# Loading and turning the first half of an attention stage by head pairs, with its hand-written order rearranged

## The chip, the cores and the metric

One core of one Trainium2 chip runs the whole program. The metric is the device time of one execution in microseconds (us); lower is better. The time before is the median of three runs, 586.37 us (585.89 to 587.06).

## The reference, cut to what is computed

Windowed attention with block summaries (2 batches, 8 heads, 768 positions, 64 numbers per head), then two feed-forward layers (1536 tokens, width 512, inner width 2048), each with its own weights.

```python
k_sum = k.reshape(B, H, 24, 32, 64).max(axis=3)       # one key per 32 positions
v_sum = v.reshape(B, H, 24, 32, 64).mean(axis=3)
scores_l = scale * q @ k.T       # only where |i - j| < 16, else -1e9
scores_s = scale * q @ k_sum.T + log(32)
a = softmax(concat(scores_l, scores_s));  x = a @ concat(v, v_sum)
h = x @ moe_w_in;   x = relu(h)**2 @ moe_w_out
h = x @ moe2_w_in;  x = h * sigmoid(1.702 * h) @ moe2_w_out
```

## The kernel before, in words

**Attention** (lines 377 to 630) works on 12 blocks of 128 query rows, six per batch, and on *units* of two blocks. In the order list each item is one letter and its numbers:

- `k,u,packed` and `q,u,packed` (`load_unit`, 377) load a unit. Packed is one DMA of 512 KB in which a partition holds two neighbouring rows of each head, so that the runs in memory are 512 bytes; unpacked is two DMAs of 256 KB with runs of 256 bytes. `kin` is a ring of three buffers, `q_ring` of two.
- `tk,u` and `tq,u` (`t_k` 489, `t_q` 528, both through `transposed` 462) turn a unit on TensorE with the 128x128 identity, eight products of 128 columns. A packed unit leaves PSUM by four copies of 64 partitions x 512, an unpacked one by two of 128 x 512. `t_k` then takes the maxima of 32 positions (into `ks`) and copies the neighbours' edges; `pk,u` (`put_ks` 519) copies the 24 maxima, once all three units of the batch are there, to both ends of each key window `kw`.
- `sv,b` (`sum_v` 440) loads v of a batch by three packed units into the `kin` ring and sums it by products with the matrix `band`. Four head pairs stand side by side in the array's columns. `ps,b` (`put_vs` 417) copies the sums `vs` into the four buffers of `vw`: two by engine copies, the other two by DMAs that GpSimd issues. `v,i` (`load_vw` 398) loads the value windows of a block, two DMAs of up to 96 partitions with runs of 256 bytes.
- `h,i,e` (`head` 535): with e = 0 the scores of all eight heads of block i (32 records at line 551), the masked minima on VectorE (565) and then the softmax of the even heads; with e = 1 the softmax of the odd heads. The exponentials (574) are on ScalarE, one instruction a head; the sum's reciprocal (588) is on VectorE, and the scaling (581) is on VectorE or GpSimd.
- `t,i` (`tail` 593) turns the probabilities (602), multiplies by the values (614) and splits the result into a rounded part `xh` and a remainder `xl`.

**The first feed-forward layer on the first 512 tokens** (blocks 0 to 3) runs inside the attention stage. `w,f,z` (`prep` 741, `fetch` 683) loads one half of weight block f (z = 0 of `w_in`, z = 1 of `w_out`; 16 blocks, 512 KB a half) and splits it into two parts on ScalarE (699, 730) and VectorE (703, 706, 735). `s,f,half` and `S,f` (`step` 758, `finish` 807) multiply half the tokens or all 512: twelve products at line 768, the activation, and twelve at line 820 into `acc`. The second half of a step is emitted behind the first half of the next one.

**What sets the order.** `ORDER` (27) is read from left to right. Each item adds its operations to `Plan` (113), which places each at the earliest free stretch of its engine (of the DMA queue, for a load) after its inputs, by costs written in the code; `soonest` (194) picks the engine that would end first. All instructions are then emitted by planned start, so that every engine runs its own in that order. An item further left has the first choice of time. `fill` (235) puts products of the identity (`keep_warm`, 1120) into TensorE's planned idle stretches before the first product into `acc3`. Behind the attention stage, `layer`, `pairs` and `late` go through the rest of the two layers.

Of the kernel before, what the change touches and what calls it, by code (L numbers as in the profile page):

```python
# [18 lines left out]
P = 128  # L19
NEG = -8.0e9  # L20

# [6 lines left out]
    m,1 k,2,1 sel w,1,0 m,0 k,1,1 q,1,1 k,0,1 tk,0 tk,1 tk,2 pk,0 q,0,1 sv,0 tq,0 h,1,0 tq,1 m,2 h,1,1 h,0,0  # L28
    w,1,1 pk,1 q,2,0 v,0 h,0,1 ps,0 h,3,0 tq,2 v,1 t,1 h,2,0 v,2 v,3 pk,2 h,2,1 t,0 h,3,1 k,3,0 t,2 s,1,0
    t,3 tk,3 w,2,0 q,3,0 tq,3 k,4,1 tk,4 w,3,0 h,4,0 s,1,1 w,3,1 h,5,0 s,3,0 k,5,0 s,3,1 w,5,0 h,5,1 w,2,1  # L30
    w,0,0 q,4,1 s,2,0 tk,5 w,5,1 S,5 w,9,0 s,2,1 w,6,0 h,4,1 pk,3 w,9,1 v,4 S,9 w,6,1 pk,5 tq,4 w,0,1 t,4
    v,5 h,7,0 w,7,0 s,0,0 t,5 w,7,1 s,0,1 w,4,0 S,7 q,5,1 w,11,0 pk,4 w,4,1 h,6,0 sv,1 S,4 h,7,1 v,6 ps,1
    w,8,0 w,11,1 tq,5 v,7 t,7 S,6 h,6,1 w,10,0 h,8,0 v,8 S,11 h,9,0 h,8,1 t,6 w,8,1 h,9,1 v,9 v,10 w,15,0
    t,8 S,8 w,10,1 S,10 w,12,0 w,12,1 w,15,1 v,11 t,9 h,10,0 w,13,0 S,12 S,15 w,14,0 h,11,0 w,13,1 h,10,1
    S,13 w,14,1 h,11,1 t,10 S,14 t,11
"""
# [219 lines left out]
def kernel(  # L256
# [73 lines left out]
    consts = Buf([], None)  # L330

# [32 lines left out]
    kw_ring = ring(attn, "kw", 4, [P, NPAIR, 2, KW])  # L364
# [12 lines left out]
    def load_unit(dst, src, ring_, u, packed):  # L377
        b, j = divmod(u, NU)
        buf = ring_.take()
        if packed:  # L380
            plan.dma(1.85, lambda: nc.sync.dma_start(
                out=buf.t.rearrange("p (h r d) -> p h r d", h=H, r=2),
                in_=src[b, :, j * UNIT:(j + 1) * UNIT, :].rearrange("h (p r) d -> p h r d", r=2)), writes=[(buf, 0)])
# [8 lines left out]
    def load_k(u, packed=False):  # L392
        load_unit(kin, k, kin_ring, u, packed)

    def load_q(u, packed=False):
        load_unit(qin, q, q_ring, u, packed)

# [63 lines left out]

    def transposed(src, dst):


        buf, packed = src
        w, at = dst
        for n in range(2):
            ps = banks.take()

            def go(n=n, ps=ps):  # L470
                for a in range(4):
                    c0 = (2 * a + n) * P if packed else (a % 2) * H * D + (2 * n + a // 2) * P
                    nc.tensor.transpose(ps.t[:, a * P:(a + 1) * P], buf.t[:, c0:c0 + P], ident)

            op("PE", 0.46, go, reads=[(buf, 0), (consts, "ident")] + ([] if packed else [(buf, 1)]), writes=[(ps, 0)])
            if not packed:
                copy(lambda n=n: at(slice(0, P), slice(2 * n, 2 * n + 2)),
                     lambda ps=ps: ps.t.rearrange("p (a i t) -> p a i t", a=2, i=2), ps, [(w, ("own", 2 * n))])
                w.writer["own", 2 * n + 1] = plan.ops[-1]
                continue  # L480
            for i in range(2):
                copy(lambda n=n, i=i: at(slice(n * D, n * D + D), slice(0, NPAIR)).rearrange(
                    "p a z (t i) -> p a z t i", i=2)[:, :, :, :, i],
                     lambda ps=ps, i=i: ps.t[i * D:i * D + D, :].rearrange("p (a z t) -> p a z t", a=4, z=2),
                     ps, [(w, ("own", 2 * n + i))], cost=0.59)

    OWNS = [("own", x) for x in range(4)]

    def t_k(u):
# [5 lines left out]
        zero = [(0, NSUM)] if j == 0 else [(1, OWN + P)] if j == NU - 1 else []  # L495
        for i, c0 in zero:
            op("POOL", 0.2, lambda i=i, c0=c0: nc.gpsimd.memset(w.t[:, :, i, c0:c0 + EDGE], 0.0),
               writes=[(w, (i, "l" if c0 == NSUM else "r"))])
        transposed(kin[u], (w, lambda rows, ps: w.t[rows, ps, :, OWN:OWN + P]))
        for z in range(2):  # L500
# [4 lines left out]
               reads=[(w, x) for x in (OWNS if kin[u][1] else OWNS[2 * z:2 * z + 2])], writes=[(ks[b], (j, z))])  # L505
# [651 lines left out]
```

## Time and profile before

| | |
|---|---|
| median of three runs | 586.37 us (585.89 to 587.06) |
| span of the profiled execution, first to last instruction | 584.6 us |
| the profiled execution's own time | no figure beside the span is given; the span is 1.8 us under the median |
| TensorE busy | 571.6 us (98%) |
| VectorE busy | 480.4 us (82%) |
| ScalarE busy | 441.8 us (76%) |
| GpSimd busy | 65.8 us (11%) |
| granted TensorE clock | 1.00 throughout (the 2.4 GHz level) |
| chain that ended last | 86% TensorE, 5% ScalarE, 4% VectorE, 3% DMA |
| moved by DMA | 95.79 MB, 164 GB/s over the span |

A busy share is an average over stages with different limits, and TensorE's includes the products of the identity. Matmul ends are modelled, so neighbouring records overlap; the distance from one start to the next tells more than a record's length. In the rows, L is a line of the kernel, `x` the number of instructions, and "idle before, releaser" what an engine waited for.

### The profile page before, as it was taken

The numbers are of one execution on the slowest core, as the hardware profiler recorded it, in microseconds if no ns is written. First come the engines' busy times: TensorE is split into PE (matmuls) and PEld (weight loads), VectorE is DVE, ScalarE is ACT, GpSimd is POOL, SyncE is SP. The second block draws the span as 40 slices with busy tenths as digits, with TensorE's granted clock in tenths as the row PEclk, the third lists the DMA queues.
The fourth block names the chain that finished last, engine by engine and source line by source line (L and its number), as shares of the span: only waits on it lengthen the run. The fifth ranks groups of instructions, "written<-read, shape, count | busy, mean of one in ns | idle before, by whom it ended". The sixth has DMA issues, their size and how long they took to land.

```text
span 584.6 us, 9824 instructions
## 1 busy us (share of the span) xinstructions
PE 571.6 (98%) x3440; PEld 474.3 (81%) x3440; DVE 480.4 (82%) x1040; ACT 441.8 (76%) x909; POOL 65.8 (11%) x125
## 2 busy tenths in 40 slices
PE   7899999999999999999999999999999999999997
PEld 6789888788878888888888888888878888888885
DVE  4899998799889998878888899899998898877421
ACT  5899889999888658888888867676587777778322
POOL 5323113112100000100000000000100002000000
PEclk9999999999999999999999999999999999999999
DMA  9999889555446624444444546633465455545001
GB/s 251 238 237 239 243 260 255 148 172 180 148 148 191 201 71 143 143 145 145 145 145 143 180 145 211 186 112 104 148 181 177 152 178 174 178 163 200 0 1 72
DMA packets 87505, 95.79 MB, mean 164 GB/s; under 512 B 29504, under 2 KB 74560, under 8 KB 87456
## 3 DMA queue, kind: packets, MB, share of 16 engines
q1 hardware_dynamic: 87264, 94.78, 54.1%
q0 software_dynamic: 192, 0.39, 0.4%
q8 instruction: 27, 0.44, 0.3%
q14 instruction: 22, 0.18, 0.1%
HBM read 91.62 MB, written 3.15 MB: 162 GB/s over the span
## 4 chain that ended last, share of the span: by engine, by line
PE 86%; ACT 5%; DVE 4%; DMA 3%; SPq 1%; issue 1%; POOL 0%; DVEq 0%; ACTq 0%
PE acc L996 13%; PE acc L820 13%; PE acc L822 11%; PE m L996 10%; PE m L822 9%; PE h L768 6%; PE m L820 6%; PE h L996 3%; PE acc L768 3%; PE m L768 3%; PE h L822 3%; PE h L820 2%; ACT sm L574 2%; PE m L614 2%; DMA kin<-in_k_dram 1%; DMA kin<-in_v_dram 1%
## 5 line engine op out<-in xcount | busy, mean ns | idle before, releaser
L730 ACT CAST w<-xw 128x512 fp32r<-128x512 f32 (+1 forms) x167 | 97.9, 602 | 20.1 <-DVE xw L706 12.8
L735 DVE TENSOR_TENSOR w<-xw,w 128x512 fp32r<-128x512 f32 (+1 forms) x163 | 107.5, 672 | 5.9 <-ACT w L730 4.0
L706 DVE SCALAR_TENSOR_TENSOR xw<-raw,xw 128x512 uint32<-128x512 uint32 x148 | 101.5, 695 | 5.6 <-ACT raw L699 1.8
L699 ACT ACTIVATE raw<-raw 128x512 f32<-128x512 f32 x148 | 96.1, 675 | 10.9 <-DMA raw<-in_moe_w_out_dram 6.3
L820 PE MATMUL acc<-gh,w 128*128 128x512 f32 (+1 forms) x288 | 82.3, 369 | 0.4 <-DVE w L735 0.2
L703 DVE TENSOR_SCALAR xw<-raw 128x512 uint32<-128x512 uint32 x148 | 65.8, 449 | 6.2 <-DMA raw<-in_moe_w_out_dram 5.8
L820 PEld LDWEIGHTS acc<-gh,w 128*128 128x128 f32 x288 | 51.7, 188 | 9.9 <-DVE w L735 0.5
L822 PE MATMUL acc<-w,gh 128*128 128x512 f32 x192 | 59.1, 389 | 0.0
L768 PE MATMUL h<-xh,w 128*128 128x512 f32 (+1 forms) x184 | 55.6, 363 | 0.6 <-DVE st L588 0.6
L820 PE MATMUL acc<-gl,w 128*128 128x512 f32 (+1 forms) x144 | 52.7, 366 | 0.0
L996 PE MATMUL acc<-top,w 128*128 128x512 f32 x192 | 48.3, 391 | 0.0
L822 PE MATMUL m<-w,gh 128*128 128x512 f32 x148 | 45.7, 390 | 0.0
L735 DVE TENSOR_TENSOR gl<-gs,gh 128x512 fp32r<-128x512 f32 x32 | 22.1, 691 | 28.5 <-ACT gh L730 27.8
L730 ACT CAST gh<-gs 128x512 fp32r<-128x512 f32 x32 | 19.9, 622 | 33.5 <-PE acc L822 25.4
L735 POOL TENSOR_TENSOR w<-xw,w 128x512 fp32r<-128x512 f32 x17 | 22.9, 1344 | 195.9 <-ACT w L730 170.2
L996 PEld LDWEIGHTS acc<-top,w 128*128 128x128 f32 x192 | 35.8, 188 | 8.5 <-ACT r L309 1.2
L822 PEld LDWEIGHTS acc<-w,gh 128*128 128x128 f32 x192 | 36.0, 188 | 7.5
L768 PEld LDWEIGHTS h<-xh,w 128*128 128x128 f32 x184 | 33.3, 189 | 6.3 <-ACT sm L574 0.8
L822 PE MATMUL acc<-w,gl 128*128 128x512 f32 x96 | 37.4, 389 | 0.0
L574 ACT ACTIVATE sm<-sm,st 128x120 f32<-128x120 f32 x96 | 36.6, 383 | 0.0
L996 PE MATMUL m<-top,w 128*128 128x512 f32 x138 | 35.0, 391 | 0.0
L996 PE MATMUL acc<-xh,w 128*128 128x512 f32 x100 | 34.0, 389 | 0.0
(188 smaller groups left out, 1201.8 us busy)
## 6 DMA issues: line engine op xcount, KB each, us to landing
raw<-in_moe_w_out_dram SPq DMA_DIRECT2D x88, 512.0 KB, 3.8
raw<-in_moe_w_in_dram SPq DMA_DIRECT2D x60, 512.0 KB, 3.9
vw<-in_v_dram SPq DMA_DIRECT2D x20, 192.0 KB, 5.8
kin<-in_v_dram SPq DMA_DIRECT2D x6, 512.0 KB, 7.0
out_dram<-r SPq DMA_DIRECT2D x12, 256.0 KB, 2.1
kin<-in_k_dram SPq DMA_DIRECT2D x4, 512.0 KB, 6.0
qin<-in_q_dram SPq DMA_DIRECT2D x4, 512.0 KB, 7.1
qin<-in_q_dram SPq DMA_DIRECT2D x4, 256.0 KB, 6.8
```

Of the source, the lines that this page charges most:

```text
L574: nc.scalar.activation(out=s.t[:, h, :], in_=s.t[:, h, :], func=AF.Exp, bias=st.t[:, 0, h:h + 1], scale=-1.0, accum_out=st.t[:, 1, h:h + 1])
L614: nc.tensor.matmul(ps.t[e * D:(e + 1) * D, p * P + c * HALF:p * P + (c + 1) * HALF], lhsT=vw[i].t[:, c, h * D:(h + 1) * D], rhs=t.t[:, h, ...
L699: nc.scalar.activation(out=top, in_=top, func=AF.Prelu, scale=-(2.0 ** -80), alpha=-(2.0 ** -32))
L703: op("DVE", 0.36, lambda: nc.vector.tensor_scalar(out=x.t, in0=raw.t[:, :, 0], scalar1=29, scalar2=None, op0=ALU.logical_shift_right), rea ...
L706: op("DVE", 0.64, lambda: nc.vector.scalar_tensor_tensor(out=x.t, in0=raw.t[:, :, 1], scalar=3, in1=x.t, op0=ALU.logical_shift_left, op1=A ...
L730: plan.soonest([("ACT", 0.09 + 0.44 * fr, False, lambda: nc.scalar.copy(out=hi.t[:, hc], in_=src())), ("DVE", 0.05 + 0.4 * fr, True, lambd ...
L735: eng.tensor_tensor(out=lo.t[:, lc], in0=src(), in1=hi.t[:, hc].bitcast(F32), op=ALU.subtract)
L768: nc.tensor.matmul(hp.t[:, cols], lhsT=w.t[:, kc * P:(kc + 1) * P], rhs=x.t[:, kc, cols], start=(kc == 0 and n == 0), stop=(kc == KC - 1 a ...
L820: nc.tensor.matmul(a.t[:, cols], lhsT=w.t[:, j * P:(j + 1) * P], rhs=g.t[:, cols], **st)
L822: nc.tensor.matmul(a.t, lhsT=g.t[:, j * P:(j + 1) * P], rhs=w.t, **st)
L996: nc.tensor.matmul(bank.t, lhsT=a, rhs=rhs(b, kh), start=(begin and k == 0 and n == 0), stop=(k == 1 and n == 2), skip_group_check=True)
```

## The change

- k of batch 0 comes as four head pairs (`K,p`, `load_kp`) in place of three units: one DMA of 393 KB, 96 partitions, each with eight neighbouring rows of two heads in runs of 2 KB. `T,p` (`t_kp`) turns a pair by two groups of eight products of 64 columns (96 moving), takes each group out by one copy of 128 x 384, forms the maxima in one reduction and writes edges and maxima for all six blocks at once. The four `kw` buffers become one tile.
- v of batch 0 for the sums comes the same way (`V,p`, `sum_vp`): four loads in the `kin` ring, each summed by eight products that follow each other in the same 24 columns, and one copy of 24 x 128. Batch 1 keeps `sv,1`.
- A new mode packed = 2 (used by `q,0,2`): two loads of four heads, turned by products of 64 columns, out by copies of 128 x 256.
- The softmax goes by two head pairs (heads 0 to 3, 4 to 7) in place of even and odd heads. `g,i,g` (`head_half`) computes the scores of two pairs alone; blocks 0 and 1 use it, the rest `h`. Buffers are tracked per pair.
- `ORDER` is another list. In it q,4 and q,5 are unpacked, k,3 and k,5 packed. The items `W`, `L` and `F` are defined and not used; with `BACK` = 6 and no `L` the later layers' order is the same as before.

```diff
 ORDER = """
+    sel selw K,3 w,3,0 m,0 m,1 m,2 K,0 K,1 q,1,1 q,0,2 T,0 w,1,0 T,3 T,1 K,2 tq,0 T,2 w,2,0 tq,1 g,0,0 g,1,0
+    V,0 g,0,1 v,0 g,1,1 h,2,0 V,1 V,2 v,1 v,2 V,3 k,3,1 ps,0 t,0 k,5,1 h,3,0 q,2,0 h,3,1 w,3,1 t,1 s,3,0
+    h,2,1 tk,3 w,1,1 v,3 t,2 t,3 w,0,0 k,4,1 w,0,1 tq,2 q,3,0 s,1,0 s,1,1 s,0,1 s,3,1 v,4 h,4,0 w,5,0 w,2,1
...
+    def load_pair(src, p):
+        buf = kin_ring.take()
+        plan.dma(1.2, lambda: nc.sync.dma_start(
+            out=buf.t[0:ROWS].rearrange("p (h x) -> p h x", h=2),
+            in_=src[0, 2 * p:2 * p + 2].rearrange("h (p r) d -> p h (r d)", r=RUN)), writes=[(buf, 0)])
...
+    def sum_vp(p):
+        buf = load_pair(v, p)
+        ps = banks.take()
+
+        def go():
+            x = buf.t[0:ROWS].rearrange("p (h r d) -> p h r d", h=2, r=RUN)
+            for r in range(RUN):
+                nc.tensor.matmul(ps.t[0:NSUM, 0:P], lhsT=band_w, rhs=x[:, :, r, :], start=(r == 0), stop=(r == RUN - 1))
...
+    def t_kp(p):
...
+        buf = kpair[p]
...
+        for g in range(2):
+            ps = banks.take()
+
+            def go(g=g, ps=ps):
+                for r in range(4):
+                    for x in range(2):
+                        c0 = (x * RUN + 4 * g + r) * D
+                        nc.tensor.matmul(ps.t[x * D:(x + 1) * D, r * ROWS:(r + 1) * ROWS], lhsT=buf.t[0:ROWS, c0:c0 + D],
+                                         rhs=ident[0:ROWS, 0:ROWS], start=True, stop=True)
...
-    def head(i, e):
+    def scores(i, gs):
...
-            for h in range(e, H, 2):
+            for h in range(4 * g, 4 * g + 4):
```

## Rows read from the trace of the kernel before

**Rows 1.** Busy time by stretch: length, then PE, PEld, DVE, ACT, POOL, clock, DMA, GB/s
```profile
0.00:13.00 13.00, 9.32 (x63) 8.65 (x64) 5.46 (x9) 6.64 (x10) 7.83 (x43) 1.00 0.95 246
13.00:20.00 7.00, 5.91 (x113) 4.54 (x116) 5.52 (x19) 5.44 (x10) 0.59 (x3) 1.00 1.19 308
20.00:36.20 16.20, 13.10 (x225) 11.61 (x217) 14.56 (x78) 15.33 (x65) 5.75 (x12) 1.00 1.10 202
36.20:45.00 8.80, 8.72 (x132) 7.87 (x136) 7.58 (x15) 8.70 (x27) 3.35 (x8) 1.00 0.95 266
45.00:84.00 39.00, 38.12 (x356) 34.14 (x345) 36.06 (x110) 35.73 (x96) 9.41 (x19) 1.00 0.87 240
84.00:165.00 81.00, 80.81 (x757) 66.16 (x756) 70.22 (x198) 71.42 (x187) 16.14 (x24) 1.00 0.64 184
```

**Rows 2.** The products of the identity, line 1123: duration, first and last start
```profile
L1123 PE MATMUL warm<-ident x80: 275/275/579, 1.4 to 35.3; 128*128 128x128 f32 x80
```

**Rows 3.** Timeline of TensorE: the first product of the feed-forward layer
```profile
36.18 0.35 PE L768 MATMUL h<-xh,w 128*128 128x256 f32 x1 [0.62 <-DVE st L588]
```

**Rows 4.** The chain that ended last, up to the first feed-forward step: start, length, what
```profile
4.03 7.92 DMA kin<-in_k_dram
...
13.11 6.01 DMA kin<-in_v_dram
...
21.01 4.54 ACT sm L574 x24
...
32.27 1.10 PE m L614 x32
...
35.34 0.69 DVE xl L627
```

**Rows 5.** The same chain further on: what one piece of TensorE's work takes
```profile
92.14 1.44 PE m L452 x48
...
111.72 2.72 PE acc L820 x12
...
145.49 0.98 PE m L551 x32
...
152.18 0.87 PE m L602 x8
...
164.88 2.72 PE h L768 x12
```

**Rows 6.** Busy time by stretch, columns as in rows 1: three stretches with few kinds of load
```profile
9.00:12.00 3.00, 1.82 (x18) 1.63 (x16) 2.74 (x5) 2.03 (x4) 0.85 (x5) 1.00 1.22 290
24.50:29.00 4.50, 4.25 (x37) 4.05 (x37) 3.64 (x9) 4.33 (x17) 1.72 (x4) 1.00 1.23 199
41.90:44.90 3.00, 3.00 (x62) 2.60 (x63) 2.43 (x5) 2.99 (x7) 1.25 (x2) 1.00 1.12 352
```

**Rows 7.** Groups by line and form, ScalarE and VectorE: busy us, mean ns, idle before
```profile
L309 ACT COPY kw<-acc 64x512 f32<-64x512 f32 x5 | 3.1, 621 | 1.5 <-PE acc L473 1.4
L309 ACT COPY qT<-acc 128x512 f32<-128x512 f32 x1 | 0.6, 585 | 0.0
L782 ACT ACTIVATE r<-h 128x256 f32<-128x256 f32 x2 | 0.8, 380 | 0.2 <-PE h L768 0.2
L502 DVE TENSOR_REDUCE ks<-kw 128x16 f32<-128x512 f32 x6 | 3.8, 681 | 0.8 <-ACT kw L309 0.7
L309 ACT COPY vs<-m 24x128 f32<-24x128 f32 x3 | 0.8, 257 | 1.8 <-PE m L452 1.4 <-DVE vs L310 0.4
L424 ACT COPY vw<-vs 24x512 f32<-24x512 f32 x1 | 0.6, 617 | 0.0
```

**Rows 8.** The page's groups by line: two of the five instructions that split a weight half
```profile
L699 ACT ACTIVATE raw<-raw 128x512 f32<-128x512 f32 x148 | 96.1, 675 | 10.9 <-DMA raw<-in_moe_w_out_dram 6.3
...
L703 DVE TENSOR_SCALAR xw<-raw 128x512 uint32<-128x512 uint32 x148 | 65.8, 449 | 6.2 <-DMA raw<-in_moe_w_out_dram 5.8
```

**Rows 9.** The page's DMA issues: KB each, median us from issue to landing
```profile
vw<-vs POOLq DMA_DIRECT2D x4, 96.0 KB, 5.5
```

More of the change, by code (lines that the diff above doesn't have):

```diff
@@ L481, in transposed @@
[L481 to L487, printed above, removed]
+                    if packed < 2:
+                        c0 = (2 * a + n) * P if packed else (a % 2) * H * D + (2 * n + a // 2) * P
+                        nc.tensor.transpose(ps.t[:, a * P:(a + 1) * P], buf.t[:, c0:c0 + P], ident)
+                        continue
@@ L574, in ex, with softmax @@
+    def softmax(i, g):
+        s, st = sms[i]
+        hs = slice(4 * g, 4 * g + 4)
+        mine = [(s, (x, g)) for x in range(2)]
+        def ex():
+            for h in range(4 * g, 4 * g + 4):
                 nc.scalar.activation(out=s.t[:, h, :], in_=s.t[:, h, :], func=AF.Exp, bias=st.t[:, 0, h:h + 1],
@@ L676, in layer @@
                 prep(m, f)
-            step(m, t, f, 0, TT, [n == 0] * 2, [n == len(order) - 1] * 2)
+            step(m, t, f, 0, TT, [fresh and n == 0] * 2, [n == len(order) - 1] * 2)
             if n >= 2:
@@ L1074, in part, with more, drain @@
         steps[:] = count
+    mores = []
+    def more(f):
+        step(1, 0, f, 0, TT, [not mores] * 2, [False] * 2)
+        mores.append(f)
+    def drain():
+        while pending:
+            finish()
     todo = dict(
-        k=load_k, q=load_q, v=load_vw, tk=t_k, tq=t_q,
+        K=load_kp, T=t_kp, V=sum_vp, g=head_half, q=load_q, k=load_k, v=load_vw, tk=t_k, tq=t_q,
         h=head, t=tail, ps=put_vs, pk=put_ks, sv=sum_v, w=lambda f, z: prep(0, f, f % RING, (z,)),
@@ L1088 @@
     used = [int(item.split(",")[1]) for item in ORDER.split() if item[:2] in ("s,", "S,")]
-    keep_w.update((0, f) for f in sorted(blocks.values(), key=lambda f: used[::-1].index(f))[:2])
+    if not any(item[:2] == "L," for item in ORDER.split()):
+        keep_w.update((0, f) for f in sorted(blocks.values(), key=lambda f: used[::-1].index(f))[:2])
     attn_ops = []
@@ L1100 @@
     end_attention()
+    if not mores:
+        drain()
+    early.clear()
     plan.lean = 1.5, 0.25
     banks.release(banks.last["h0"])
-    while pending:
-        finish()
     parted.add((0, 0))
@@ L1108 @@
     two = list(range(NF))
-    layer(1, 0, two[:1:-1][:10], operands_first(0, 1, 2, *one[:2]))
+    rest = [f for f in two[:1:-1] + two[1::-1] if f not in mores]
+    layer(1, 0, rest[:-BACK], operands_first(0, 1, 2, *one[:2]), not mores)
     pairs(0, 1, 2, one)
```

219 lines of the change are left out of this document (149 added, 70 removed).

## The prediction

> **What bounds the kernel now.** I read the busy time by stretch first. From 36.2 us on TensorE idles for almost nothing: 8.72 of 8.80 us, 38.12 of 39, 80.81 of 81 [rows 1]. Part of what stands before that is no work: the products of the identity run from 1.4 to 35.3 us [rows 2]. The first product of the feed-forward layer starts at 36.18 us [rows 3]. So the total is roughly that moment, plus the useful TensorE work still open at it, plus the holes in what follows.
>
> The holes I get from the prices of single pieces, since records overlap. Tile 0 of the first layer is 16 steps of 2 x 2.72 us [rows 5], 87.0 us. After 36.2 there remain eight of twelve blocks' scores at 0.98 (7.8), 20 of 24 groups of turned probabilities at 0.87/2 (8.7), ten products with the values at 1.10 [rows 4] (11.0), six units of k and q (48 products of 128 columns, which I price as those of the probabilities, 0.109 each: 5.2) and batch 1's sums, 1.44 [rows 5]. That is 121.1 us. The next layer's first product starts at 164.88 [rows 5], 128.7 us after 36.18, so some 7.6 us are holes or overhead. Half steps and switches of array shape explain part, so I count at most 5 us as recoverable.
>
> VectorE and ScalarE are nearly full as well: 14.56 and 15.33 of 16.2 us between 20.0 and 36.2, still about nine tenths later [rows 1]. In the first 20 us they stand: ScalarE works 12.1 us of them, VectorE 11.0 [rows 1]. There the chain waits for loads: the third k unit lands at 11.95 us and the third v unit at 19.12, and the exponentials run from 21.01 [rows 4]. The queue is the reason: in 9 to 12 us, packed loads alone, it moves 290 GB/s, and the stretch of 256-byte runs 199 [rows 6].
>
> **The change, part by part.** *Loads.* A unit of 524 kB takes 524/290 = 1.81 us, a weight half at the rate of the weights' stretch (352 GB/s) 1.49 us, the value windows of an inner block, 393 kB in two loads, at 199 GB/s 1.98 us [rows 6]. A 2 KB run is in no load of before. Its bounds: the packed rate would give 393/290 = 1.36 us for a pair, the weights' 1.12, and the only loads with 96 partitions, those of 256-byte runs, 1.98 [rows 6]. I take 1.12, because the weights' runs (1 and 4 KB) enclose 2 KB. Eight pairs then cost 9.0 us where six units cost 10.9.
>
> *When the last v pair lands.* Before, four units and one weight half (8.7 us of moving) end at 11.95 [rows 4], so the queue starts 3.2 us late. In the new list V3 comes behind seven pairs, three weight halves, q1 and q0, and the windows of blocks 0 to 2 (three times 1.98, less 0.2 for the cut edge of the first: 5.8). With V3 this is 9.0 + 4.5 + 3.6 + 5.8 = 22.9, and V3 lands at 26.1 us, seven later than v before. K2 and the v pairs wait on SyncE for slots of the ring of three, and the loads listed behind them wait too. K2's slot is free once K3 is turned, V0's and V1's once K0 and K1 are, several loads before their turn, so I cost this at nothing; a queue that ran dry would show the 3.2 us of its start again. SyncE issues three loads more in all (two k and v pairs, a half of q0; the four units that change form cancel), beside transfers that last longer.
>
> *From V3 to the first step.* Eight products that no longer stand side by side are 16 records of 0.109 (1.7 us), the copy 0.26, two rounds of copies into `vw` at 0.6 [rows 7] (GpSimd, VectorE and ScalarE share them): 29.3 us. From the first product with the values to the first step it was 36.18 - 32.27 = 3.9 us [rows 3, 4]. So the first step starts at 33.2 us by this chain. If the engines rather than V3 set it, later: I take 33.6, a gain of 2.6 us.
>
> *Copies.* Twelve copies of 64 x 512 at 0.62 (7.4 us) become eight of 128 x 384, between 0.38 and 0.585 [rows 7], say 0.49: 3.9. For q0 four at 0.62 become four at 0.38: 1.0 saved. The reductions move the same elements (six of 0.68 against four, which I put at 1.0), and eight small copies of maxima replace six: nothing. Some 4.5 us of two full engines are saved. GpSimd, 7.83 of the first 13 us busy [rows 1], gets three instructions for `band_w` and copies edges eight times instead of ten; the first edges are wanted near 12 us, so this costs nothing either. Softmax by pairs keeps every instruction and its shape; the packed and unpacked units change places and cancel. Products of 64 columns cost TensorE two records where a turned block had one, at most 16 x 0.109 = 1.7 us a group of a pair; these lie where the identity products lie now [rows 2] and cost nothing, while one of them late on K1 would delay the first scores by about 1 us.
>
> *Scores earlier.* The first scores need K0, K1 and half of q0, the sixth load: 3.2 + 3 x 1.12 + 1.49 + 1.81 + 0.91 = 10.8 us, against 13.8 for all of k, q1 and q0 before. With turning and maxima, exponentials can start near 14.5 instead of 21.01. This fills the empty first 20 us of ScalarE, and it is why I think that V3 and not the softmax comes last before the first tail.
>
> *What is given back.* q2 is turned before 36.2 now, and after the first step in the new list: 8 x 0.109 = 0.9 us of TensorE work, as said. With the load order it is also later. Blocks 2 and 3 use the sums that GpSimd's DMAs bring 5.5 us after their issue [rows 9]: from about 28.1, so near 34; that half of the tokens can be ready near 39, and is not what holds the steps.
>
> *Holes.* With 4.5 us less on two full engines and a queue that moves k and v of batch 0 in 1.9 us less, I take back 1.0 of the 5 us.
>
> *Sum.* -2.6 + 0.9 - 1.0 = -2.7 us on a span of 584.6: 581.9. The median of the runs stands 1.8 us above that span, and I put the difference on it: 586.4 - 2.7 = **583.7 us**. Both ends: a first step at 33.2 with all holes gone gives -3.0 + 0.9 - 5.0 = -7.1; the load at 1.98 us makes V3 6.9 us later, and -2.6 + 0.9 + 6.9 = +5.2.
>
> **The rivals.** *Slower: the pair loads leave part of the queue's engines without work.* A pair fills 96 of 128 partitions. If the moving went by partitions, it would run at three quarters of the rate: 1.12/0.75 = 1.49 us a pair, 8 x 0.37 = 3.0 us later for V3, and -2.6 + 0.9 + 3.0 = +1.3 without the gain in holes: 587.7 us. It decides from 1.33 us a pair on, where 8 x 0.21 eats the 1.7. For it: the loads of 96 partitions were in the slowest stretch, 199 GB/s. Against it: these have 256-byte runs, which explains the rate, and the queue's busy share there is no lower (1.23) than for packed loads (1.22) [rows 6]. The Trainium skill, page "DMA: Bandwidth & Descriptors", section "Rules for kernel authors", asks for 128 partitions and at least 1 MiB in a DMA for full bandwidth, which speaks against loads of 96 partitions and 393 kB. The same page, on why a DMA increments its semaphore by 16, lets a tile of 96 partitions use all 16 engines, and by that part the pair costs 1.12; the equal busy shares fit it.
>
> *The same: weights are late.* At the first step only first halves (w3, w1, w2) are there. The second half of block 3 comes behind V3, k3, k5, q2 (2.6 us at 199 GB/s) and itself: 26.1 + 1.8 + 1.8 + 2.6 + 1.5 = 33.8 us, and its split is five instructions of 0.45 to 0.7 [rows 8], so 37 us on full engines. Between 33.6 and 37 TensorE then has twelve half products of two steps, q2, k3 and the tails. If these are not ready either, 2 to 3 us of new holes take the gain: 586.2 us. For it: the engines are full at that time; against it: five pieces of other work stand in the list there.
>
> *Much faster: the holes go.* If ScalarE and VectorE are what makes the holes, starting their work six us earlier closes them: the -7.1 above, 579.3 us, and up to 581.9. Against it: the splits and exponentials left are the same, and after 84 us both engines have slack [rows 1] and TensorE has not.
>
> **How the numbers follow.** The forecast, a gain of 1.3 to 4.5 us, 0.44; much faster 0.17; the same 0.21; slower 0.18. A difference of 0.2% (1.2 us) is about what a measurement can tell. So faster 0.61, same 0.21, slower 0.18. The range leaves out a tenth at each end: 580.0 to 588.3, which takes in the pair load at 1.5 us and most of the closed holes; 1.98 us a pair lies outside.
>
> **What would show it.** Right: V3's eight products start near 26 us, the first product of the feed-forward layer (line 768 now) starts at 33 to 34.5 us, and TensorE idles no more after it than now; the stretch of k pairs shows well over 290 GB/s. Exponentials begin near 14.5 us. Wrong: V3 after 28 us; a first step after 35 us; or identity products gone earlier but holes of over 2 us between 34 and 45 us, with splits of weights as releasers. If the first step comes before 32 us and the total does not follow, supply and not the start was the bound.

## The result, and the profile after

The changed kernel takes **590.59 us** (median of four runs, 589.69 to 591.61), against 586.42 of the kernel before in the same session: the ratio is 1.0065 with a 95% interval of [1.0047, 1.0083]. The profiled execution took 590.84 us, its span is 588.9 us. Slower by 4.2 us where 2.7 us of gain were forecast, and outside the range.

The busy time by stretch, columns as in [rows 1]:

```profile
0.00:13.00 13.00, 11.03 (x104) 10.29 (x106) 3.88 (x7) 4.86 (x8) 8.50 (x43) 1.00 0.93 240
13.00:20.00 7.00, 6.83 (x117) 5.76 (x114) 4.61 (x22) 5.59 (x12) 0.44 (x2) 1.00 1.15 243
20.00:36.20 16.20, 13.03 (x175) 10.75 (x174) 12.37 (x69) 12.48 (x57) 2.92 (x10) 0.94 1.19 216
36.20:45.00 8.80, 8.05 (x109) 7.53 (x109) 6.41 (x14) 8.13 (x26) 3.90 (x9) 0.92 1.10 237
```

VectorE and ScalarE work *less* up to 36.2 us than before (20.9 and 22.9 us against 25.5 and 27.4 of [rows 1]). The 4.5 us of copies that the prediction saves are about half of this; for the rest, they have not got what they should work on. While K0 and K1 land, the queue moves 258 GB/s, where well over 290 was the sign that the prediction is right:

```profile
8.30:9.90 1.60, 1.60 (x21) 1.52 (x22) 1.11 (x2) 0.24 (x1) 1.18 (x5) 1.00 1.16 258
```

The chain that ended last, from the first v pair on (start, length, what; a DMA's length is from issue to landing, and the loads queued ahead of it land within it):

```profile
11.25 10.09 DMA kin<-in_v_dram
...
26.14 7.08 DMA kin<-in_v_dram
...
33.27 2.82 PE acc L496 x16
```

In [rows 4] the third v unit had landed at 19.12 us. Here the fourth v pair is issued at 26.14 and its products (line 496) start at 33.27. TensorE's timeline shows what this makes of the two moments on which the sum was built, the first product of the feed-forward layer (line 884 now; [rows 3]) and the next layer's first:

```profile
4.47 1.55 PE L562 MATMUL acc<-ident,kin 96*64 96x96 f32 x16 [0.54 <-DMA kin<-in_k_dram]
8.38 2.83 PE L562 MATMUL acc<-ident,kin 96*64 96x96 f32 x32
18.19 0.88 PE L562 MATMUL h<-ident,kin 96*64 96x96 f32 x16
18.90 0.83 PE L562 MATMUL acc<-ident,kin 96*64 96x96 f32 x16
33.27 2.82 PE L496 MATMUL acc<-kin,band_w 96*24 96x128 f32 x16 [2.06 <-DMA kin<-in_v_dram]
43.88 0.39 PE L884 MATMUL h<-xh,w 128*128 128x256 f32 x1
...
169.41 0.39 PE L884 MATMUL h<-xh,w 128*128 128x512 f32 x1
```

The next layer's first product in the kernel before:

```profile
164.72 0.39 PE L768 MATMUL h<-xh,w 128*128 128x512 f32 x1
```

The first product comes at 43.88 instead of 36.18 (+7.7), the next layer at 169.41 instead of 164.72 (+4.7; the chain's piece of it, 164.88 in [rows 5], starts 0.2 later than the first record). Between the two moments lie 125.5 us now, 128.5 before: three of the 7.7 us come back. Twelve more products that turn probabilities are done by then (64 left of 96 where 76 were left; 12 x 0.109 = 1.3 us), and the rest is fewer holes. From the next layer's first product to the end it is 419.5 us, before 419.9. So in this execution the whole loss arises ahead of the first feed-forward product. The longest waits there of ScalarE, VectorE and TensorE all go back to the last v pair (waits from 20 to 45 us: engine, line, what for; total, times, longest):

```profile
ACT vs L310 <- PE acc L496: 3.0, 1, 3.0
DVE vw L451 <- ACT vs L310: 3.0, 1, 3.0
PE acc L496 <- DMA kin<-in_v_dram: 2.1, 1, 2.1
```

Two theories stood against each other. **Loads:** a load on 96 partitions takes longer than one on 128 whatever its runs, and eight of them put the last v pair off. **Clock:** there are 24 products of the identity left where 80 stood [rows 2]; 32 records of line 562 take 2.83 us at 8.38 us, at the lower level (1.2 GHz), and 1.5 us at 18.19 at the upper (2.4 GHz); and the windows show 0.94 and 0.92 from 20 to 45 us, where the engine had just idled 2.06 us for the last v pair. (The windows print 1.00 from 0 to 13 us all the same, and so does the table of the kernel before; the lengths of the records tell otherwise. An identity product takes 421 ns or more up to 8.03 us here, and mostly 275 from 19.9 on. In the kernel before, 14 of them stand without a gap up to 4.36 us, 421 ns or more each, and from 6.07 on they take 275.) Two more were tried: that an earlier start is lost to late weights anyway (**supply**), and that the **list** does not fit.

### The profile page after: what moved, and what is told of

Read it like the earlier page. It is cut to its first block, busy times and chain, and to the rows that moved or that the text cites. A ratio compares the mean times of both kernels' runs of the same rounds, so it can differ in the third digit from the quotient of the medians.

```text
span 588.9 us, 9991 instructions
## 1 busy us (share of the span) xinstructions
PE 578.0 (98%) x3528; PEld 481.1 (82%) x3528; DVE 480.5 (82%) x1043; ACT 439.1 (75%) x906; POOL 61.7 (10%) x122
## 4 chain that ended last, share of the span: by engine, by line
PE 91%; DMA 5%; ACT 1%; DVE 1%; issue 0%; POOL 0%; POOLq 0%; DVEq 0%
PE acc L936 13%; PE acc L1112 13%; PE acc L938 11%; PE m L1112 10%; PE m L938 9%; PE h L884 8%; PE m L936 6%; PE h L1112 4%; PE acc L884 3%; DMA kin<-in_v_dram 3%; PE m L884 3%; PE h L938 3%; DMA raw<-in_moe_w_in_dram 2%; PE h L936 2%; PE m L729 2%; PE m L717 1%
## 5 line engine op out<-in xcount | busy, mean ns | idle before, releaser
L850 DVE TENSOR_TENSOR w<-xw,w 128x512 fp32r<-128x512 f32 (+1 forms) x171 | 115.3, 683 | 6.7 <-ACT w L845 3.5
L821 DVE SCALAR_TENSOR_TENSOR xw<-raw,xw 128x512 uint32<-128x512 uint32 x148 | 102.7, 699 | 7.6 <-ACT raw L814 3.5
L818 DVE TENSOR_SCALAR xw<-raw 128x512 uint32<-128x512 uint32 x148 | 63.6, 435 | 12.9 <-DMA raw<-in_moe_w_in_dram 10.2
L1112 PE MATMUL acc<-top,w 128*128 128x512 f32 x186 | 47.1, 391 | 0.0
L845 ACT CAST gh<-gs 128x512 fp32r<-128x512 f32 x32 | 19.9, 623 | 35.0 <-PE h L938 25.4
L938 PE MATMUL acc<-w,gl 128*128 128x512 f32 x96 | 37.4, 389 | 0.0
L884 PE MATMUL h<-xl,w 128*128 128x512 f32 (+1 forms) x92 | 32.5, 353 | 0.0
```

Source lines behind the costliest of these rows:

```text
L818: op("DVE", 0.36, lambda: nc.vector.tensor_scalar(out=x.t, in0=raw.t[:, :, 0], scalar1=29, scalar2=None, op0=ALU.logical_shift_right), rea ...
L821: op("DVE", 0.64, lambda: nc.vector.scalar_tensor_tensor(out=x.t, in0=raw.t[:, :, 1], scalar=3, in1=x.t, op0=ALU.logical_shift_left, op1=A ...
L845: plan.soonest([("ACT", 0.09 + 0.44 * fr, False, lambda: nc.scalar.copy(out=hi.t[:, hc], in_=src())), ("DVE", 0.05 + 0.4 * fr, True, lambd ...
L850: eng.tensor_tensor(out=lo.t[:, lc], in0=src(), in1=hi.t[:, hc].bitcast(F32), op=ALU.subtract)
L884: nc.tensor.matmul(hp.t[:, cols], lhsT=w.t[:, kc * P:(kc + 1) * P], rhs=x.t[:, kc, cols], start=(kc == 0 and n == 0), stop=(kc == KC - 1 a ...
L938: nc.tensor.matmul(a.t, lhsT=g.t[:, j * P:(j + 1) * P], rhs=w.t, **st)
```

## The experiments

All medians against the kernel before on the same chip; since that one takes 586.4 to 587.5 us there, the ratios compare better than the medians. "V" is where the last v sum's products start, "first" the first feed-forward product, "next" the next layer's first, each in us of the profiled execution. That execution lies within 1.6 us of its median, except in v6_same, where it is 2.7 us above it.

| run | what differs from the changed kernel | median | ratio, 95% interval | V | first | next |
|---|---|---|---|---|---|---|
| (changed) | | 590.59 | 1.0065 [1.0047, 1.0083] | 33.3 | 43.9 | 169.4 |
| v_first | v pairs listed ahead of the windows | 591.92 | 1.0090 [1.0059, 1.0122] | 26.7 | 38.9 | 170.0 |
| v_units | v of batch 0 in three units | 590.25 | 1.0055 [1.0038, 1.0072] | 25.7 | 36.7 | 168.8 |
| v_units_w31 | the same, one weight half earlier | 591.26 | 1.0074 [1.0050, 1.0098] | 25.9 | 36.7 | 168.6 |
| old_list | the order of before, so no pair load at all | 589.37 | 1.0035 [1.0019, 1.0050] | 20.3 | 40.7 | 168.4 |
| dense | denser products of the identity | 590.35 | 1.0059 [1.0036, 1.0082] | 33.9 | 43.1 | 168.0 |
| k_units | k of batch 0 in three units | 591.75 | 1.0065 [1.0042, 1.0088] | 31.0 | 42.8 | 169.3 |
| price | pair load planned at 1.6 us | 592.65 | 1.0095 [1.0071, 1.0120] | 34.0 | 41.7 | 170.8 |
| refit_pairs | pair load planned at 1.7 us, list rearranged | 593.63 | 1.0121 [1.0088, 1.0155] | 31.1 | 40.9 | 172.2 |
| refit_units | no pair load, list rearranged | 588.87 | 1.0028 [1.0013, 1.0043] | 29.3 | 42.1 | 167.2 |
| v6 | v pairs on 128 partitions | 587.12 | 1.0011 [0.9990, 1.0031] | 30.5 | 39.3 | 165.6 |
| v6_same | the same, and the plan of the changed kernel | 585.38 | 0.9976 [0.9965, 0.9987] | 32.8 | 41.6 | 166.7 |
| v6_dense | v6_same with denser products of the identity | 585.46 | 0.9973 [0.9961, 0.9985] | 29.5 | 38.2 | 162.6 |
| refit_v6 | v pairs on 128 partitions, list rearranged | 584.97 | 0.9967 [0.9953, 0.9981] | 27.9 | 36.6 | 163.4 |
| refit_v6_dense | the same with denser products | 584.82 | 0.9972 [0.9961, 0.9983] | 28.8 | 37.4 | 163.0 |

**Loads alone.** Two kernels of nothing but loads, twelve of a form in a row.

```diff
+FORMS = [(8, 128, 128, "r512p128"), (8, 96, 128, "r512p96"), (2, 128, 512, "r2kp128"), (2, 96, 512, "r2kp96"),
+         (1, 128, 1024, "r4kp128"), (1, 96, 1024, "r4kp96"), (16, 128, 64, "r256p128"), (16, 96, 64, "r256p96")]
...
+            nc.sync.dma_start(out=t[0:p].rearrange("p (x r) -> p x r", x=x),
+                              in_=flat[o0:o0 + x * p * r].rearrange("(x p r) -> p x r", x=x, p=p))
```

> Only loads: twelve each of eight forms, runs of 512 B, 2 KB, 4 KB and 256 B, each on 128 partitions (512 KB) and on 96 (384 KB); the attention and both layers are left out and the output is zeros. Partition theory (96 of 128 partitions leave part of the queue idle): every form takes the same time on 96 as on 128 partitions, so the pair form (2 KB, 96) takes what 2 KB on 128 takes, about 1.4 us. Run theory (the runs alone set the rate): the 96 form takes 0.75 of the 128 form, the pair form about 1.1 us. Contention theory (the pair load is slow only beside other loads): the pair form alone takes 1.1 us as well, and the 1.4 to 2.0 us between landings in the changed kernel come from its neighbours.

Busy time by stretch, each stretch inside one form, in the order of the list (length, VectorE, GpSimd, clock, DMA share, GB/s):

```profile
7.00:20.00 13.00, 1.23 (x8) 0.00 (x0) 1.00 1.15 346
23.00:36.00 13.00, 1.47 (x10) 0.00 (x0) 1.00 1.24 279
41.00:54.00 13.00, 1.54 (x10) 0.00 (x0) 1.00 1.05 404
57.00:70.00 13.00, 1.36 (x10) 0.00 (x0) 1.00 1.06 278
74.00:86.00 12.00, 1.39 (x9) 0.00 (x0) 1.00 1.03 416
90.00:102.00 12.00, 1.35 (x9) 0.00 (x0) 1.00 1.02 281
108.00:124.00 16.00, 1.23 (x8) 0.00 (x0) 1.00 1.20 272
130.00:140.00 10.00, 0.93 (x7) 0.00 (x0) 1.00 1.17 256
```

On 128 partitions (every other row) the rate follows the run: 272 GB/s with 256 bytes, 346 with 512, 404 with 2 KB, 416 with 4 KB. On 96 it stays near 280 from 512 bytes on: the 2 KB runs buy nothing. And the DMA share is the same for both, 1.05 at 404 GB/s and 1.06 at 278. The pair form takes 393/278 = 1.41 us with nothing beside it, so the run theory and the contention theory, which expected 1.1, fail. What was expected of the partitions, the same time on 96 as on 128, holds at 2 KB roughly (1.41 us against 524/404 = 1.30), and not with 256 bytes (393/256 = 1.54 against 524/272 = 1.93). Each load kernel ran once. Later the second kernel, with the pair as it is, the same 393 kB on 128 partitions, the packed unit and half a block's windows:

```diff
-FORMS = [(8, 128, 128, "r512p128"), (8, 96, 128, "r512p96"), (2, 128, 512, "r2kp128"), (2, 96, 512, "r2kp96"),
-         (1, 128, 1024, "r4kp128"), (1, 96, 1024, "r4kp96"), (16, 128, 64, "r256p128"), (16, 96, 64, "r256p96")]
+FORMS = [(2, 96, 512, "pair96"), (2, 128, 384, "pair128"), (8, 128, 128, "unit"), (8, 96, 64, "window")]
```

> Loads alone, twelve in a row of each form, everything else left out (the output is zeros): a pair on 96 partitions with runs of 2 KB, the same 393 kB on 128 partitions with runs of 1.5 KB, a packed unit of 524 kB, and value windows (96 partitions, 256-byte runs, 196 kB). Load theory: 1.4 us a load for the first, 0.95 to 1.05 for the second (390 to 410 GB/s), 1.5 for the unit, and under 0.85 for the windows. Rival, the bytes set the time: the first two agree within 5%.

VectorE's timeline, a copy behind each load, two neighbours of each form (the difference of their starts is one load):

```profile
9.40 0.15 DVE L31 COPY acc<-pair 96x1 f32<-96x1 f32 x1 [1.47 <-DMA pair<-in_k_dram]
11.06 0.15 DVE L31 COPY acc<-pair 96x1 f32<-96x1 f32 x1 [1.51 <-DMA pair<-in_k_dram]
...
26.45 0.15 DVE L31 COPY acc<-pair 128x1 f32<-128x1 f32 x1 [0.90 <-DMA pair<-in_k_dram]
27.49 0.15 DVE L31 COPY acc<-pair 128x1 f32<-128x1 f32 x1 [0.89 <-DMA pair<-in_k_dram]
...
40.33 0.15 DVE L31 COPY acc<-unit 128x1 f32<-128x1 f32 x1 [1.65 <-DMA unit<-in_k_dram]
42.14 0.15 DVE L31 COPY acc<-unit 128x1 f32<-128x1 f32 x1 [1.65 <-DMA unit<-in_k_dram]
...
61.97 0.15 DVE L31 COPY acc<-window 96x1 f32<-96x1 f32 x1 [0.88 <-DMA window<-in_k_dram]
63.00 0.15 DVE L31 COPY acc<-window 96x1 f32<-96x1 f32 x1 [0.88 <-DMA window<-in_k_dram]
```

Over the twelve it is mostly 1.64 us for the pair, 1.05 for the same bytes on 128 partitions, 1.81 for the unit (which is what it took in the kernel before, [rows 6]), 1.03 for half a block's windows. Pair and unit are 16 and 20% slower than in the first load kernel, which ran on another chip (393/278 = 1.41 and 524/346 = 1.51), so only ratios within one run count: four pairs cost 6.6 us where three units cost 5.4.

**The order of the v loads.** First the v pairs before the value windows, then v in units.

```diff
-    V,0 g,0,1 v,0 g,1,1 h,2,0 V,1 V,2 v,1 v,2 V,3 k,3,1 ...
+    V,0 V,1 V,2 V,3 g,0,1 v,0 g,1,1 h,2,0 v,1 v,2 k,3,1 ...
```

> The changed kernel with its four v pairs listed together ahead of the value windows. Order theory (V3 is late because the windows of blocks 0 to 2 and the slots stand before it): V3 lands 4 to 5 us sooner than 33.2, the first feed-forward product starts near 40 instead of 43.9, total 587 us. Load theory (the pair loads themselves are slow): V3 lands sooner too, but by less than 3 us since V1 to V3 still wait for slots, and the windows land later; total 588.5 to 590.5.

```diff
-    V,0 g,0,1 v,0 g,1,1 h,2,0 V,1 V,2 v,1 v,2 V,3 k,3,1 ...
+    sv,0 g,0,1 v,0 g,1,1 h,2,0 v,1 v,2 k,3,1 ...
```

> The changed kernel with v of batch 0 by the three packed units and the band sums of before, at the place of the first v pair. Load theory: three units at 1.81 replace four pairs at 1.5 to 1.7, the last lands near 26 us, its sum takes 0.64 instead of 2.8, the first feed-forward product starts by 38, total 585 to 587 us. Order theory: as v_first within 1 us, since both have v ahead of the windows.

Both bring the first product forward, by 5.0 and 7.2 us, and both give it back: the next layer comes 131.1 and 132.2 us after it. Neither total was expected by any theory: v in units, its last sum at 25.7 us, is as slow as the changed kernel. The waits of TensorE in v_units, from 36 to 48 us, are on the value windows and on copies of k:

```profile
PE m L729 <- DMA vw<-in_v_dram: 1.2, 2, 0.6
...
PE acc L515 <- DVE kw L311: 0.8, 1, 0.8
```

So an early start alone is worth nothing here. Whether one weight half is the cause was tried next.

```diff
-    ... tq,0 T,2 w,2,0 tq,1 ... h,3,1 w,3,1 t,1
+    ... tq,0 T,2 w,3,1 tq,1 ... h,3,1 w,2,0 t,1
```

> The kernel with v of batch 0 in packed units (it reached the first feed-forward product at 36.7 us and gave all of it back in holes), now with the second half of weight block 3 listed where the first half of block 2 stood, and the other way round. Supply theory (the holes after an early first step are products that wait for second halves): the second product group of block 3 starts before 41 us instead of 47, the next layer begins at 166 to 167 us instead of 168.84, the median is 587.5 to 588.5. Rival, the list as a whole (every engine's order is placed for other costs, no single load is the cause): the next layer stays at 168.5 or later and the median at 590 or above.

Next layer 168.6 and a median of 591.26, as the rival said: this load is not the cause of the holes. Other single loads were not tried, and what would close them stays open.

**The order of before.**

```diff
-    sel selw K,3 w,3,0 m,0 m,1 m,2 K,0 K,1 q,1,1 q,0,2 T,0 w,1,0 T,3 T,1 K,2 tq,0 T,2 w,2,0 tq,1 g,0,0 g,1,0
+    m,1 k,2,1 sel w,1,0 m,0 k,1,1 q,1,1 k,0,1 tk,0 tk,1 tk,2 pk,0 q,0,1 sv,0 tq,0 h,1,0 tq,1 m,2 h,1,1 h,0,0
```

> The changed kernel with the list of the kernel before: no pair loads, no products of 64 columns, only the softmax by pairs and the finer tracking remain. If these cost nothing: 586.4 within 0.2%. If the softmax by pairs costs time (the first turned group needs both banks' minima), 587.5 or more.

Without any pair load the new code is still 0.35% slower under the old list, about half of the changed kernel's loss. What is left of the change there is the softmax by two pairs, the tracking of buffers per pair and `kw` as one tile, and with them another order on every engine; which of these costs the time was not separated.

**The clock.**

```diff
-            for n in range(int((a - t - 0.3) * 0.75 / dur)):
+            for n in range(int((a - t - 0.1) / dur)):
...
-                o.eng, o.fn, o.seq, o.far, o.start = "PE", fn, len(self.ops), False, t + n * dur / 0.75
+                o.eng, o.fn, o.seq, o.far, o.start = "PE", fn, len(self.ops), False, t + n * dur
```

> The changed kernel, only with the products of the identity planned without gaps between them in every planned idle stretch (before, a quarter of each stretch was left free). Clock theory (the half level of the granted clock until 13.65 us and from 34.1 to 37.5 us, which falls on the turning of the k pairs and on the sum of the last v pair, makes part of the loss): the clock is at its full level before 9 us and through the sum of the last v pair, whose eight products take 1.6 us instead of 2.82; the first feed-forward product comes at 42 to 43 us instead of 43.88, and the median falls by 1.0 to 1.5 us, to about 589.3. Load theory (the pair loads alone): the last v pair still lands at 33, the median stays at 590.3 to 590.8. If the clock rises and the total stays, holes after the first step take it back.

The turning of the second pair falls from 2.83 to 1.54 us and the last v sum from 2.82 to 1.93, but it still starts at 33.90:

```profile
8.05 1.54 PE L562 MATMUL acc<-ident,kin 96*64 96x96 f32 x32 [0.28 <-DMA kin<-in_k_dram]
...
33.90 1.93 PE L496 MATMUL acc<-kin,band_w 96*24 96x128 f32 x16 [0.99 <-DMA kin<-in_v_dram]
...
43.05 0.39 PE L884 MATMUL h<-xh,w 128*128 128x256 f32 x1
```

The ratio stays where it was (1.0059 against 1.0065), though the intervals would hide a gain of 1 us. That the last sum starts no earlier fits: it waits for its load, which lands at 33.85.

This run also tells why the exponentials came late. With the clock up the scores start at 14.30 us, 2.3 us earlier, and still the first exponential (line 680) comes at 22.14. ScalarE runs its own in the planned order, and ahead of the exponentials stand copies of the pair K2, which lands only at 18.5, and splits of weights (TensorE, then ScalarE):

```profile
18.54 1.32 PE L562 MATMUL h<-ident,kin 96*64 96x96 f32 x16 [2.19 <-DMA kin<-in_k_dram]
```
```profile
21.18 0.48 ACT L310 COPY kw<-acc 128x384 f32<-128x384 f32 x1 [0.80 <-PE acc L562]
21.56 0.68 ACT L814 ACTIVATE raw<-raw 128x512 f32<-128x512 f32 x1
22.14 0.38 ACT L680 ACTIVATE sm<-sm,st 128x120 f32<-128x120 f32 x1
```

**Prices and k.**

```diff
-        plan.dma(1.2, lambda: nc.sync.dma_start(
+        plan.dma(1.6, lambda: nc.sync.dma_start(
```

> The changed kernel with the planned price of a pair load at 1.6 us instead of 1.2, nothing else. The order in which each engine runs its work follows from the planned prices. Theory that the plan, placed for loads that are too cheap, puts work that waits for the v pairs ahead of work that is ready: the median falls by 1 us or more, below 589.6, with the first feed-forward product at 42 us or earlier. Load theory (the loads are late whatever the plan): 590 to 591, the first feed-forward product at 43 to 45 us.

```diff
-    sel selw K,3 w,3,0 m,0 m,1 m,2 K,0 K,1 q,1,1 q,0,2 T,0 w,1,0 T,3 T,1 K,2 tq,0 T,2 w,2,0 ...
+    sel selw k,2,1 w,3,0 m,0 m,1 m,2 k,1,1 k,0,1 q,1,1 q,0,2 tk,0 w,1,0 tk,1 tq,0 tk,2 pk,0 pk,1 pk,2 w,2,0 ...
```

> The changed kernel with k of batch 0 by three packed units of 512 kB and 128 partitions again, the v pairs kept. Load theory: by the loads alone three units take 3 x 1.50 = 4.5 us of the queue against 4 x 1.39 = 5.6 for the pairs, so the last v pair lands 1 us or more earlier (its sum starts near 32 instead of 33.27) and the median falls by 0.5 to 1.5 us, to about 589.5. Rival, the copies: the twelve copies of 64 x 512 come back in place of eight of 128 x 384 (3.5 us of two full engines), and the time is 591 to 593.

No gain from either. With the list as it is, k in units changes nothing that can be told (1.0065 in both), though the last v sum starts 2.3 us earlier; a truer price alone is, if anything, slower (1.0095, intervals that overlap). So the list was rearranged for the true price, and beside it one for the code without pair loads.

```diff
-        plan.dma(1.2, lambda: nc.sync.dma_start(
+        plan.dma(1.7, lambda: nc.sync.dma_start(
```

> The changed kernel with the pair load planned at 1.7 us, and the list rearranged (items moved one by one, a move kept when the plan's own end comes earlier) for that price: the plan ends at 587.9 us, against 592.6 with a price of 1.6 and the old list, 584.9 for the changed kernel as it was planned and 588.1 for the kernel before. Theory that the list was fitted to loads that are too cheap, and the pair loads in themselves cost about what they save: 586 to 588.5, no difference from before, 2 to 4 us under the changed kernel. Rival, the pair loads cost their time under any list: 590 or more.

> The changed code without a single pair load: k and v of batch 0 in units, as before, softmax by two head pairs, and a list rearranged in the same way from the list of before: the plan ends at 585.3 us (588.1 for the kernel before, 593.3 for the changed code with the list of before, which measured 589.4). If the plan is as good a guide here as for the kernels with units so far (measured 1.7 to 3.9 us under the planned end): 581.5 to 583.6, faster than both. Rival, the earlier plan is lost to holes on the chip as in the kernels with an early first step: 586 or more.

In both the rival named beforehand held: the plan's own end, 587.9 and 585.3 us, is no guide to tenths of a per cent. With the pair loads the other list is slower still; its last v sum starts at 31.06 us:

```profile
31.06 1.93 PE L496 MATMUL m<-kin,band_w 96*24 96x128 f32 x16
```

And the code without pair loads stays slower than before under either list.

**The form of the v loads alone.** Six neighbouring rows of two heads on each of 128 partitions, the same bytes; the sum is six products with a band for each row.

```diff
-        buf = load_pair(v, p)
+        buf = kin_ring.take()
+        plan.dma(1.2, lambda: nc.sync.dma_start(
+            out=buf.t[:, 0:2 * RV * D].rearrange("p (h x) -> p h x", h=2),
+            in_=v[0, 2 * p:2 * p + 2].rearrange("h (p r) d -> p h (r d)", r=RV)), writes=[(buf, 0)])
...
-            for r in range(RUN):
-                nc.tensor.matmul(ps.t[0:NSUM, 0:P], lhsT=band_w, rhs=x[:, :, r, :], start=(r == 0), stop=(r == RUN - 1))
+            for r in range(RV):
+                nc.tensor.matmul(ps.t[0:NSUM, 0:P], lhsT=band_w[:, r, :], rhs=x[:, :, r, :], start=(r == 0), stop=(r == RV - 1))
...
-        op("PE", 1.75, go, reads=[(buf, 0), (consts, "band_w")], writes=[(ps, 0)])
+        op("PE", 1.35, go, reads=[(buf, 0), (consts, "band_w")], writes=[(ps, 0)])
```

> The changed kernel and its list, with each v pair of batch 0 loaded on all 128 partitions, six neighbouring rows of two heads (runs of 1.5 KB) in a partition, in place of eight rows on 96; its sum is six products in place of eight, with a band for each row. Same 393 kB. Load theory (96 partitions move at 280 GB/s, 128 at 337 to 406): a v pair takes 1.0 to 1.2 us of the queue instead of 1.4 to 2.0, so the last one lands 1.5 to 2.5 us earlier, at 31 to 31.7 instead of 33.2, and its sum takes 12 records instead of 16; the first feed-forward product at 41 to 42 us, the median 588 to 589.5. Rival, the 1.5 KB runs or other traffic set the rate: the last pair lands at 33 or later, the median stays at 590 or more.

The loss is gone, more than expected. But the shorter planned sum also changes the plan. With the last hunk left out the plan, and so the order on every engine, is that of the changed kernel:

> As the run with the v pairs on 128 partitions, but its sum planned at the old price, so that the plan is that of the changed kernel to the last placement and every engine runs the same order; only the form of the four v loads differs, and six products in place of eight in each sum. Load theory: the last v pair lands near 28 to 30 us in place of 33.2, its sum starts there, the first feed-forward product at 38 to 40, and the median is 586.5 to 588. Rival, the other order made the gain: 589.5 to 590.6.

**585.38 us, 5.2 us less, by the form of four loads and their sums (and the band that the sums use); nothing else differs.** So the form of the v loads, with its sums, is worth the whole loss at this order. How much of it the sums alone give no run separates: their records take 5.8 us in place of 8.4 in the two profiled executions. The profiled execution is the slowest of the twelve (588.09 us). In it the last v pair lands at 30.2 us, 3.0 earlier, yet its sum starts only at 32.8, and the execution shows what comes last there: the k pairs and q0 are turned at the lower clock, the first exponential comes at 23.0 us, and VectorE works through to 34.5 (chain of waits):

```profile
8.72 2.83 PE acc L565 x32
11.55 2.56 PE m L565 x32
14.11 1.05 PE acc L518 x4
```

**The clock once more.** With the identity products denser:

> The run with the v pairs on 128 partitions and the changed kernel's plan, with the products of the identity planned without gaps, as in the first dense run. Clock theory, second part: with the v pairs on time the turning of the k pairs at the half level is what comes last; with it at the full level a group of 16 records takes 0.7 to 0.9 us instead of 1.3 to 1.5, the first exponential comes before 20 us, the first feed-forward product before 40, and the median falls by 0.5 to 2 us, to 583.4 to 584.9. Rival: VectorE's amount of work and not its late start sets the first product: no change, 585 to 586.

```profile
8.52 1.54 PE L565 MATMUL acc<-ident,kin 96*64 96x96 f32 x32
9.89 1.49 PE L565 MATMUL m<-ident,kin 96*64 96x96 f32 x32
...
29.46 1.49 PE L499 MATMUL acc<-kin,band_w 128*24 128x128 f32 x12
...
38.17 0.39 PE L887 MATMUL h<-xh,w 128*128 128x256 f32 x1
```

The profiled execution (584.39 us) does as expected, its first exponential at 19.4 us, and the median does not move (585.46, in the rival's range): over twelve runs the clock is no second part of the loss.

With dense, this run makes a second pair in which only the form of the v loads, with its sums, differs. By the ratios it is worth 5.0 us (1.0059 and 0.9973), and here the profiles show the way of it: the last v pair lands at 27.8 us in place of 33.85, its sum starts at 29.5 in place of 33.9, the first feed-forward product at 38.2 in place of 43.1, the next layer's at 162.6 in place of 168.0. The sums' records are 1.8 us shorter in all (5.8 against 7.5). Between 20 and 34 us the queue moves 264 GB/s, in dense 217 (busy time by stretch, dense first):

```profile
20.00:34.00 14.00, 13.01 (x183) 11.35 (x180) 11.35 (x62) 12.36 (x55) 2.70 (x9) 0.92 1.13 217
```
```profile
20.00:34.00 14.00, 13.55 (x216) 11.77 (x218) 13.47 (x72) 13.46 (x61) 3.88 (x10) 1.00 1.02 264
```

**A list for the better form.** k pairs planned at 1.7 us, v pairs on 128 partitions at 1.3, a list rearranged anew for these, and once more with denser products of the identity:

> The kernel with the k pairs at 1.7 us, the v pairs on 128 partitions at 1.3 us, and a list rearranged for these: the plan ends at 586.8 us. If the pair loads are the whole loss and the list follows the true prices: 584.5 to 587, at or under the kernel before and 1 us under the rearranged kernel with both pairs on 96 partitions. Rival, as there: 590 or more.

> The kernel with the v pairs on 128 partitions and its own rearranged list (584.97), with the products of the identity planned without gaps. Its profiled execution shows the clock at the full level throughout and the first exponential at 14.7 us, so the clock theory expects no change: 584.3 to 585.3. If it falls as far as the other kernel does, the products of the identity act otherwise than by the clock while k is turned.

584.97 and 584.82: 0.3% under the kernel before, and the lowest medians here, though not told apart from v6_same.

## Why the prediction was wrong, point by point

**The step that failed is the price of a pair load.** "A 2 KB run is in no load of before … I take 1.12, because the weights' runs (1 and 4 KB) enclose 2 KB." It went by the run, and on 96 partitions runs from 512 bytes to 4 KB all give about 280 GB/s. By itself a pair takes 1.64 us where the unit takes its 1.81. Eight pairs are then 13.1 us instead of 9.0, "Eight pairs then cost 9.0 us where six units cost 10.9" turns round, and V3 at 26.1 becomes 30.2. It landed at 33.2. Two of the remaining 3 us had arisen ahead of the v pairs: the third weight half (w2) lands at 19.9 us, where the same sum with 1.64 us a pair gives 3.2 + 4 x 1.64 + 3 x 1.49 + 3.6 = 17.8. From one landing to the next the three weight halves take 2.0, 2.1 and 2.6 us, and why was not separated. From w2 to V3 it is 13.3 us, and 12.4 by the prices of single loads (four pairs at 1.64, and the 5.8 that the prediction gives the windows). With the v pairs on 128 partitions this stretch shrinks by 2.6 us (v6_same) and by 3.3 (v6_dense against dense), where the four loads are 4 x 0.59 = 2.4 us cheaper by themselves. So there the price of a single load accounts for most of it.

**The rival that names it** was there, "the pair loads leave part of the queue's engines without work", with 1.49 us a pair and 587.7 us. Its effect is borne out, and is larger than it said (1.64 against 1.05 us for the same bytes, where three quarters of the rate would give 1.40); its time fell short by 2.9 us. Its reason, engines of the queue without work, is not shown. It was put at 0.18 because "the queue's busy share there is no lower (1.23) than for packed loads (1.22) [rows 6]". That share says nothing of it: in the load kernel it is 1.05 and 1.06 at 404 and 278 GB/s. The Trainium skill, page "DMA: Bandwidth & Descriptors", section "Rules for kernel authors", asks for 128 partitions; the load kernels agree, 404 against 278 GB/s. What the same page of the Trainium skill states where it tells why a DMA increments its semaphore by 16, that a tile of 96 partitions uses all 16 engines, was the wrong thing to price a load by: in the load kernels no stretch of such loads shows more than 281 GB/s. How the packets are shared out among the engines no run here shows.

**From V3 to the first step.** 7.5 us were counted, 10.7 passed (33.22 to 43.88). The eight products took 2.82 us instead of 1.7 (1.93 in dense, at the upper clock), at the lower clock, right behind a wait of 2.06 us; and TensorE runs in order, so the turning of k3 and of other blocks stood behind the wait and then ahead of the first product.

**Exponentials near 14.5 us.** They began at 20.98, as in the kernel before (21.01 in [rows 4]). K0, K1, q1 and half of q0 were there by 12.4 us, but turning these two pairs took 5.3 us at the lower clock (8.38 to 13.70), and the scores started at 16.62. The prediction took the identity products for no work; that they keep the clock up was not priced. Yet this alone did not hold the exponentials: in dense the clock is up, the scores start at 14.30, and the first exponential comes at 22.14. The prediction went by what the first scores need; in the list's order ScalarE first takes the copies of K2 and splits of weights, which wait for their loads. Another list reaches 14.7 (refit_v6).

**What is given back, and holes.** Together -0.1 us was forecast for the work after the first step; it was -3.0. The sign was right by luck: it was forecast from copies and loads saved, and it came from the first step's own lateness, since 1.3 us more of turned probabilities had been done by then and fewer holes followed. The prediction's sign "If the first step comes before 32 us and the total does not follow, supply and not the start was the bound" was never met, but v_units is like it: a first step at 36.7 us was no gain. Up to the next layer TensorE's waits in v_units are for value windows, copies of k and results of VectorE in the tails, none of them for a weight; the one weight half that was moved changed nothing, and so the rival "the same: weights are late" is not shown.

**Copies.** Right: the copies of 128 x 384 took 0.48 us where 0.49 was put (changed kernel, groups by line and form: min, median, max in ns):

```profile
L310 ACT COPY kw<-acc x4: 479/480/486, 6.1 to 20.0; 128x384 f32<-128x384 f32 x4
L562 PE MATMUL acc<-ident,kin x64: 246/367/423, 4.5 to 19.5; 96*64 96x96 f32 x64
L1256 PE MATMUL warm<-ident x24: 275/421/582, 1.4 to 42.3; 128*128 128x128 f32 x24
```

No run shows them to be worth anything here: k_units, with the old copies of k and cheaper loads, has the same ratio. The products of 64 columns stayed under the bound of 1.7 us a group of 16: 0.71 at the upper clock (18.19 to 18.90), 1.33 at the lower (4.47 to 5.80; records of 367 and 246 ns, the identity product's 421 and 275). But they were not hidden, since what came first waited for them.

With the true load price alone the prediction's own sum gives 583.7 + 8 x 0.52 = 587.9 us, inside its range. In its own terms the whole miss adds up in the profiled executions: the last v pair 7.1 us later than counted, the way from it to the first step 3.2 longer, the work up to the next layer 2.9 shorter, and 0.4 gained behind that. From -2.7 this makes +4.3, the difference of the two spans.

Two things stay open. The code without any pair load is 0.3% slower than before under either list, for a reason that was not found. And v in units, whose last sum is there 7.5 us earlier than in the changed kernel, gains nothing, while v pairs on 128 partitions gain 5 us: so what the form of the v loads is worth was shown for the changed kernel's order, and not for others.

## What to carry to other kernels

Price a load first by its partitions and then by its run: laying the same bytes over all 128 partitions was worth more here (1.05 against 1.64 us) than any run length on 96. Before believing a plan, time each new form of load by itself; and when two variants differ in planned costs, keep the plan fixed and change the form alone, since a greedy plan reorders every engine and moves the time on its own (by 2.0 us between v6 and v6_same, which differ in one planned cost). An earlier start of the bound stage counts only if what it uses next is there.

## What was not expected of the hardware

- The rate on 96 partitions hardly depends on the run from 512 bytes on: 278 to 281 GB/s with 512 bytes, 2 KB and 4 KB, against 346 to 416 on 128. With 256-byte runs it is 256 against 272.
- The same form moves at other rates in other executions: a packed unit at 346 GB/s in the first load kernel and at 290 (524/1.81) in the second, on another chip, which was the rate in the kernel before too.
- Two products of 64 columns into the two halves of the partitions overlap: their records start 0.044 us apart (0.71/16) with 96 columns moving, those of the turned probabilities 0.109 (0.87/8, [rows 5]) with 128. That is 0.46 and 0.85 ns a moving column, both at the upper clock.
